# A recurrent-memory attention block on one core: steps padded to 3072 TensorE instructions per four, a transpose moved to DMA, and two reorderings at the last step

## The chip, the cores and the metric

The kernel runs on one core of one Trainium2 chip. The metric is the device time of one execution in microseconds; the kernel before takes 1007.62 us (median of three runs, 1007.40 to 1008.14). TensorE holds 128 x 128 cells. A product whose stationary operand has 32 columns uses a 128 x 32 strip of it, here called a tile; the four tiles 0, 32, 64 and 96 write the partitions 0-31, 32-63, 64-95 and 96-127 of a PSUM bank and can work side by side.

## What is computed

Two blocks run one after the other on x (2048 rows of 640). The first is attention over 64 segments of 32 rows; each segment sees its own rows and 8 memory rows, and its first 8 output rows are the memory of the next segment, so that the segments form a chain. The second is a gated feed-forward block.

```python
h = concat([mem, layernorm(x)[32*s : 32*s+32]])      # 40 rows
q, k, v = h @ Wq, h @ Wk, h @ Wv                     # 32 heads of 128
p = softmax(mask(q @ k.T * 128**-0.5))
o = (p @ v) @ Wo                                     # 40 rows of 640
mem, out[s] = o[:8], o[8:]
...
h = x + out
y = h + (relu(n @ W_gate) * (n @ W_up)) @ W_down     # n = layernorm(h), 1728 wide
```

## The kernel before, in words

**How it is written.** The code records operations in program order with what each reads and writes; `_Graph.solve` derives the waits. Within an engine the order is the written one, so nothing is scheduled: the order of the calls is the order of the instructions on each engine. An operation of TensorE ("pe") may hold many products.

**TensorE instructions.** `pe.matmul` makes two instructions, a weight load and a product. `again` (L357) makes a product without a load: it uses the weights that stand in the tile. One 32-column load with one 512-column product is the unit of the projections.

**A step.** The loop `for s in range(1, NSEG)` (L927) does segment s. `project` (L365) multiplies the 32 rows that are new to the step (8 of memory, 24 of x) by a half of Wk, Wq or Wv: five chunks c of 128 input features, and for each chunk four products of 512 columns, one on each tile (g = 0 to 3). `halves` says which half of the heads, `chunks` which chunks in which order, `ends` the chunks with which the PSUM sum starts and stops, and `held` that the first chunk uses `again`, since the half before has ended with the same weights. A step is, in order on TensorE:

1. K in two halves into banks P2 and P3 (L946), `pv_x` of step s-1 (32 small products, L654), Q in two halves into P0 and P1 (L967);
2. V half 0 with the scores of heads' half 0 between its chunks, V half 1 with the scores of half 1 (L979 to 1012; scores are 40-column products, L466);
3. `pv_mem` 0 (L519), `filler(0)`, `pv_mem` 1, `filler(1)`;
4. `wo_split` (32 products of 320 columns, L582), `wo_pass` (64 products of 160 columns, L565), which give the next step's memory, and `filler(2)`.

The fillers are work that does not hang on the chain. In the three steps with s % 4 = 2, 3, 0 they are a projection of other rows (`PARTS`); in the steps with s % 4 = 1 from 5 to 57 they are `woe_pass` (64 load-and-product pairs of 320 columns, L625, cut into 28, 8 and 28 by `WPARTS`). Step 62 has the latter too.

**LayerNorm 1.** Every fourth step (s % 4 = 1) the next normalised 128 rows are turned from rows to columns. For full blocks a transposing DMA on SP's queue does it (`flip_rows`, L347, issued at L991). The last block has 64 rows, in step 57: there TensorE turns them (`ln1_trans`, five loads and five products, L352) into bank BQ[1], and ScalarE copies them out (L1044). GpSimd then spreads them over the steps' operands (`ln1_back`).

**The last step.** Step 63 has no Q projection. After V half 1 it issues `merge_v` (the DMAs that arrange V for `pv_x`), the exponentials and the mask, `gate_up(0, 0)` (the feed-forward block's first two groups of five full-width products, L841), the scores of half 1, and leaves the loop (L996 to 1008). Behind the loop stand `rows(P3, ...)` (64 pairs of L625 for the rows of step 62, with a copy, a sum and two DMAs), `gate_up(0, 1)` and `pv_x` (L1167 to 1170). `gate_up` number i of block 0 writes banks i % 2 and 2 + i % 2; P3 is bank 7 and T0 bank 2.

Of the kernel before, what the change touches and what calls it, by code (L numbers as in the profile page):

```python
# [163 lines left out]
def build_kernel(nc, A_x, A_mem0, A_Wq, A_Wk, A_Wv, A_Wo, A_seg_len, B_W_gate, B_W_up, B_W_down, out):  # L164
    _, S, D = A_x.shape
# [6 lines left out]
    DC = D // 128  # L172
# [86 lines left out]
    def bank_bf(b):  # L259
        return ps[:, b * 512:(b + 1) * 512].bitcast(BF16)  # L260
# [14 lines left out]
    def B(n):  # L275
        return ("B", n)
# [68 lines left out]
    def flip_rows(dst, src, skey, dkey):  # L345

        add("sp", lambda e: e.dma_start_transpose(dst, src[:, :]), r=[skey], w=[dkey], dma=True)  # L347
# [14 lines left out]
            stop_tensor_calc=stop, tile_size=(128, 32 if g is not None else 128), tile_position=(0, 32 * (g or 0)),  # L362
            bass_skip_group_check=True, ldweights=False))

    def project(act, akeys, j, halves, banks, chunks=range(5), ends=(0, DC - 1), held=False):  # L365
        swap = 1 if j == 2 and akeys[0][0] == "acte" else 0

        def f(pe):
            for c in chunks:
                for n, i in enumerate(halves):  # L370
                    for g in range(4):
                        o = 2048 * i
                        w = (W[:, j, c, o + 512 * (g ^ swap):o + 512 * (g ^ swap) + 512] if j == 2 else
                             W[:, j, c, o:o + 2048].rearrange("p (h e) -> p h e", e=128)[:, :, 32 * g:32 * g + 32])
                        a = (bank(banks[n])[32 * g:32 * g + 32, :], act[:, c, :], w)
                        if n == 0 and not (held and c == chunks[0]):
                            ins = pe.matmul(*a, start=(c == ends[0]), stop=(c == ends[1]), skip_group_check=True)  # L377
                        else:
                            ins = again(pe, *a, c == ends[0], c == ends[1], g)
            return ins  # L380
        add("pe", f, r=list(akeys) + [("W", j, c) for c in chunks], w=[B(b) for b in banks] + [("Wdone", j)])
# [23 lines left out]
    def n_rows(b):  # L405
        return 64 if b < 0 else min(128, S - 64 - 128 * b)

    def ln1_load(b, buf, key, eng="sp"):
        t0, n = (0, 64) if b < 0 else (64 + 128 * b, min(128, S - 64 - 128 * b))
        dma(buf[0:n, :], x_ap[t0:t0 + n, :], w=[key], eng=eng)  # L410

    def ln1_trans(b, buf, key, bk):
        transpose_rows(buf, key, 64 if b < 0 else min(128, S - 64 - 128 * b), bk)
# [20 lines left out]
    def chunks_of(flat):  # L434
        return flat.rearrange("p (c t) -> p c t", t=128)
# [4 lines left out]
    def pass_act(s):  # L440
        p, j = place(s)
        return act_r[p][:, j], [("act", p, j, "m"), ("act", p, "x", j), ("act", p, "x")]
# [50 lines left out]
    def exp_x(s, hf):  # L493
        _, j = place(s)
        add("act", lambda a: a.activation(ap(Px, 128 * hf, [[256, 2], [32, 4], [1, 32]]), s_view(hf, M, M + SEG),
                                          ACTF.Exp, scale=SCALE), r=[B((P0, P1)[hf])], w=[("Px", hf)])
# [425 lines left out]
    row_stats(xl, ("xl",), n_rows(1))  # L922
    row_scale(xl, ("xl",), n_rows(1), xl, ("xl",))

    WAYS = ((range(DC),), (range(DC - 1, -1, -1), (DC - 1, 0), True))

    for s in range(1, NSEG):  # L927
        last = s == NSEG - 1
# [14 lines left out]
                woe_pass(BQ[0], WPARTS[n])  # L943
        if s > 0:
            a, ks = pass_act(s)
            for i in range(2):  # L946
                project(a, ks, 1, (i,), ((P2, P3)[i],), *WAYS[i])
                to_tok((P2, P3)[i], i, "act")
                if last and i == 1:
                    load_piece(("Ko", 0), "act")  # L950
                flip(i, Ko, i, [("Ko", i)])
            if s % 4 == 2 and more:
                row_std(n_rows(nb + 1))
                row_scale(xl, ("xl",), n_rows(nb + 1), xl, ("xl",), "pool")
            if s % 4 == 1 and e2 is not None:
                row_std(128)
                row_scale(xt, ("xt",), 128, xt, ("xt",), "pool")
            pv_x(s - 1, 0)
            norm_x(0)
            if s % 4 == 0 and e2 is not None:  # L960
                add_attn(xt[:, :], xt, at, [("xt",), ("at",), ("rx",)], [("xt",)], "pool")
                dma(h_d[128 * e2:128 * e2 + 128, :], xt[:, :], r=[("xt",)], w=[("h_d", e2)])
            if s % 4 == 2:
                merge_v(s, 1)
            if not last:
                for i in range(2):
                    project(a, ks, 0, (i,), ((P0, P1)[i],), *WAYS[i])  # L967
                    to_tok((P0, P1)[i], 2 + i, "act")
                    flip(2 + i, Qo, i, [("Qo", i)])
                    if i == 0:  # L970
                        norm_x_late(0)
                        flip_ox(s - 1, (0,))
            else:
                norm_x_late(0)
                flip_ox(s - 1, (0,))
            if s == NSEG - 2:
                dma(xn2T[0][:, :, :], xn2_d[:, :, :], r=[("xn2_d", u) for u in range(4)] + [("Wdone", 0)],
                    w=[("xn2", 0, u) for u in range(4)])
            project(a, ks, 2, (0,), (P2,), range(4), held=not last)  # L979
            scores(s, 0, (0, 1))  # L980
            project(a, ks, 2, (0,), (P2,), (4,))
            scores(s, 0, (2, 3))
            if not last:
                exp_mem(s, 0)
                mask_mem(s, 0)
            to_v(P2, Vp, 0, ("Vp",), "act")
            if last:
                load_piece(("Vp", 0), "act")
            if s % 4 == 1 and ln:
                if n_rows(nb) == 128:  # L990
                    flip_rows(chunks_of(at[:, :]), xl, ("xl",), ("at",))  # L991
                else:
                    ln1_trans(nb, xl, ("xl",), BQ[1])
                if more:
                    ln1_load(nb + 1, xl, ("xl",))
        if last:  # L996
            project(a, ks, 2, (1,), (P3,))
            to_v(P3, Vp, 1, ("Vp",), "act")
            merge_v(s, 0)
            flip_ox(s - 1, (1,))  # L1000
            exp_x(s, 0)
            gate_up(0, 0)
            scores(s, 1)
            exp_x(s, 1)
            load_piece(("g1", 0), "act")
            mask_x(s)
            late_o(s - 1)
            break
        project(a, ks, 2, (1,), (P3,), range(4))
        scores(s, 1, (0, 1))  # L1010
        project(a, ks, 2, (1,), (P3,), (4,))
        scores(s, 1, (2, 3))
        flip_ox(s - 1, (1,))
        if s == NSEG - 2:
            load_piece(("Pm", 0))
# [23 lines left out]
        if s > 0 and not woe and s != NSEG - 3:  # L1039
            late_o(s - 1)  # L1040
        if s % 4 == 1 and ln:
            n = n_rows(nb)
            if n < 128:
                copy_op("act", chunks_of(at[:, :])[:, :, 0:n], chunks_of(bank_bf(BQ[1])[:, 0:D])[:, :, 0:n], [B(BQ[1])],  # L1044
                        [("at",)])
            ln1_back(nb, chunks_of(at[:, :]), [("at",)], "pool")
        mask_x(s)
        if e2c is not None:
# [115 lines left out]
    def rowbuf(p):  # L1164
        return bass.AP((xl, xt)[p], 0, [[D, 64], [1, 320]])

    rows(P3, s % 2, s - 1)  # L1167
    gate_up(0, 1)
    load_piece(("hT", 0, 0))
    pv_x(s, P0)  # L1170
    norm_x(P0)
    norm_x_late(P0)
# [110 lines left out]
```

## Time and profile before

| | |
|---|---|
| three runs | 1007.40, 1007.62 and 1008.14 us |
| profiled execution | 1006.39 us |
| its span, first to last instruction | 1004.7 us; what lies around it is 1.69 us |
| TensorE products | 971.1 us busy, 97% of the span, 25153 instructions |
| TensorE weight loads | 495.7 us, 23308 instructions |
| VectorE, ScalarE, GpSimd | 712.9, 524.7 and 167.4 us |
| loop from the first `pv_x` to that of step 63 | 59.3 to 823.2 us |

The page gives each engine's busy time, the chain of work that ended last, the DMA queues and the costliest groups. A row of a group or of the timeline names the line, the operation and the tensors, with the number of instructions that follow each other (x20), their start and length, and in brackets the idle time of the engine just before and what ended it; "issue" there means that the profile shows nothing the engine waited for. Weight loads (PEld) have rows of their own and overlap products. Ends of products are modelled, so that busy rows overlap and starts are the better measure. The queue that the page calls "instruction" carries the program's own code to the engines.

### The profile page before, as it was taken

Reading aid. Unit: us, or ns where it says so; the run is one execution under the profiler, and the core shown is the slowest. Engines: PE = TensorE matmul, PEld = TensorE weight load, DVE = VectorE, ACT = ScalarE, POOL = GpSimd, SP = SyncE. Lnnn points to the kernel's source line nnn. Section 1 sums busy time; section 2 is a strip of 40 time slices with the busy share of each in tenths; the row PEclk is TensorE's granted clock in tenths of the full one; section 3 lists DMA queues with packets and bytes.
Section 4 is the critical chain, followed back from the end, with each engine's and each line's share of the span. In section 5 each row is a group of like instructions: output and inputs, shape, how many; then the busy total and the mean of one; then the engine's idle time right before and its main releaser. Section 6 shows DMA issues by size and latency. Waiting matters only on the chain.

```text
span 1004.7 us, 53813 instructions
## 1 busy us (share of the span) xinstructions
PE 971.1 (97%) x25153; PEld 495.7 (49%) x23308; DVE 712.9 (71%) x1863; ACT 524.7 (52%) x1331; POOL 167.4 (17%) x416
## 2 busy tenths in 40 slices
PE   3789999999999999999999999999999999999998
PEld 0245555555555554555555555555555555344443
DVE  2568787878878887888788878787878765445332
ACT  0456566556666666666666666665656643122121
POOL 7020202121302130222022212111110010000000
PEclk9999999999999999999999999999999999999999
DMA  9931212121212111121212131211111158413100
GB/s 373 418 102 28 53 28 55 33 55 50 53 41 54 49 53 47 47 54 47 53 41 63 47 55 40 41 41 38 40 29 40 38 165 251 108 20 92 27 14 26
DMA packets 72421, 73.01 MB, mean 73 GB/s; under 512 B 41632, under 2 KB 59008, under 8 KB 70272
## 3 DMA queue, kind: packets, MB, share of 16 engines
q1 hardware_dynamic: 70064, 68.27, 23.6%
q8 instruction: 190, 3.11, 1.3%
q10 hardware_dynamic: 2128, 1.31, 0.5%
q14 instruction: 39, 0.32, 0.1%
HBM read 37.04 MB, written 6.55 MB: 43 GB/s over the span
## 4 chain that ended last, share of the span: by engine, by line
PE 93%; SPq 3%; DMA 2%; issue 1%; DVE 1%; ACT 0%; POOL 0%; DVEq 0%; ACTq 0%
PE ps L377 43%; PE ps L841 11%; PE ps L359 10%; PE ps L565 7%; PE ps L582 6%; PE ps L625 4%; SPq L324 3%; PE ps L1088 3%; PE ps L466 2%; PE ps L654 2%; DMA Wo<-in_A_Wo_dram 2%; PE ps L519 2%; PE ps L854 0%; PE ps L1100 0%; DVE TBf L605 0%
## 5 line engine op out<-in xcount | busy, mean ns | idle before, releaser
L377 PE MATMUL ps<-W,act_r 128*32 128x512 bf16 x6832 | 447.4, 380 | 3.1 <-DVE act_r L606 1.8
L377 PEld LDWEIGHTS ps<-W,act_r 128*32 128x32 bf16 x6832 | 169.7, 96 | 212.0 <-issue 63.1
L401 ACT ACTIVATE tok<-ps 128x512 bf16<-128x512 f32 x190 | 109.3, 594 | 57.3 <-PE ps L377 48.8
L377 PE MATMUL ps<-W,act_e 128*32 128x512 bf16 x1224 | 120.0, 383 | 8.0 <-DMA W<-in_A_Wv_dram 3.7
L396 DVE STREAM_TRANSPOSE Ko<-tox 128x512 bf16<-128x512 bf16 x128 | 89.8, 703 | 42.7 <-ACT tox L401 41.5
L474 POOL COPY Qo<-Qe 128x256 bf16<-128x256 bf16 x64 | 28.0, 437 | 528.9 <-DVE oT L539 521.0
L401 ACT ACTIVATE tox<-ps 128x512 bf16<-128x512 f32 x134 | 79.6, 598 | 56.5 <-PE ps L377 35.5
L545 DVE STREAM_TRANSPOSE oT<-tox 128x512 bf16<-128x512 bf16 x128 | 89.8, 702 | 0.0
L396 DVE STREAM_TRANSPOSE Qo<-tok 128x512 bf16<-128x512 bf16 x124 | 85.6, 690 | 0.9
L565 PE MATMUL ps<-Wo,oT 128*32 128x160 bf16 x4032 | 82.3, 233 | 2.8 <-DMA Wo<-in_A_Wo_dram 1.7
L359 PE MATMUL ps<-W,act_e 128*32 128x512 bf16 x856 | 84.6, 385 | 0.0
L582 PE MATMUL ps<-Wo,oT 128*32 128x320 bf16 x2016 | 79.8, 299 | 0.5 <-DVE rm L529 0.5
L359 PE MATMUL ps<-W,act_r 128*32 128x512 bf16 x808 | 79.9, 382 | 0.0
L565 PEld LDWEIGHTS ps<-Wo,oT 128*32 128x32 bf16 x4032 | 71.8, 97 | 12.0 <-DMA Wo<-in_A_Wo_dram 2.8
L401 ACT ACTIVATE Vp<-ps 128x512 bf16<-128x512 f32 x127 | 75.2, 592 | 0.5 <-ACT Vp L401 0.5
L869 ACT ACTIVATE g<-ps 128x512 bf16<-128x512 f32 x52 | 30.1, 593 | 79.5 <-PE ps L841 79.5
L595 ACT ACTIVATE SA<-TA 64x40 f32<-64x40 f32 x126 | 29.5, 234 | 77.0 <-DVE TA L593 76.2
L841 PE MATMUL ps<-xn2T,Wu 128*128 128x512 bf16 x259 | 64.5, 379 | 0.1
L870 DVE TENSOR_TENSOR hT<-g,ps 128x512 bf16<-128x512 bf16 x52 | 35.7, 687 | 40.6 <-PE ps L841 38.6
L482 ACT ACTIVATE Pm<-ps 128x64 bf16<-128x64 f32 x126 | 28.1, 223 | 69.2 <-PE ps L466 69.2
L841 PE MATMUL ps<-xn2T,Wg 128*128 128x512 bf16 x247 | 61.8, 379 | 1.3 <-issue 1.0
L582 PEld LDWEIGHTS ps<-Wo,oT 128*32 128x32 bf16 x2016 | 53.9, 97 | 16.0 <-DVE rm L529 1.2
(116 smaller groups left out, 1463.1 us busy)
## 6 DMA issues: line engine op xcount, KB each, us to landing
VM<-Vp SPq DMA_DIRECT2D x126, 65.0 KB
VM<-Vp SPq DMA_DIRECT2D x63, 130.0 KB
W<-in_A_Wk_dram SPq DMA_DIRECT2D x5, 1024.0 KB
W<-in_A_Wq_dram SPq DMA_DIRECT2D x5, 1024.0 KB
W<-in_A_Wv_dram SPq DMA_DIRECT2D x5, 1024.0 KB
Wo<-in_A_Wo_dram SPq DMA_DIRECT2D x8, 640.0 KB
attn_d<-wtok SPq DMA_DIRECT2D x248, 7.5 KB
xt<-in_A_x_dram SPq DMA_DIRECT2D x16, 160.0 KB
```

What stands on the lines that cost most here:

```text
L324: add(eng, lambda e: e.dma_start(dst, src), r=r, w=w, dma=True)
L359: return pe.add_instruction(mybir.InstMatmult(name=nc.get_next_instruction_name(), engine=mybir.EngineType.PE, ins=[pe.lower_ap(rhs), pe.l ...
L377: ins = pe.matmul(*a, start=(c == ends[0]), stop=(c == ends[1]), skip_group_check=True)
L396: add("dve", lambda v: v.transpose(dst[:, 16 * i:16 * i + 16, 0:32], tok[t][:, :].rearrange("p (h f) -> p h f", f=32)), r=tok_keys(t), w=keys)
L401: add("act", lambda a: a.activation(dst, src, ACTF.Copy), r=r, w=w)
L545: add("dve", lambda v, kh=kh: v.transpose(ap(oT[p], 160 * kh + M, [[320, 4], [40, 4], [1, 32]]), ap(tox, 128 * kh, [[256, 4], [1, 4], [4, ...
L565: i = pe.matmul(bank(bk)[32 * gg:32 * gg + 32, 0:160], src[:, hb, 0:32], w[:, gg], start=(hb == CH[16 * halves[0]]), stop=(hb == CH[-1]), ...
L582: i = pe.matmul(bank(bk)[32 * q:32 * q + 32, 0:320], src[:, hb, 0:32], w, start=(n == 0), stop=(n == 7), skip_group_check=True)
L625: ins = pe.matmul(bank(bk)[32 * q:32 * q + 32, 0:320], src[:, hb, 0:32], w[:, 2 * (q % 2):2 * (q % 2) + 2], start=(i == 0), stop=(i == 15) ...
L841: ins = pe.matmul(bank(bk), w[:, c, lo:lo + 128], xn2T[par][:, c, :], start=(c == 0), stop=(c == DC - 1))
L870: add("dve", lambda v: v.tensor_tensor(hT[par][:, j, :], g1[gi][:, :], bank(bu), ALU.mult), r=[B(bu), ("g1", gi)], w=[("hT", par, j)])
L1088: i = pe.matmul(*a, start=(j == 0), stop=(j == FC - 1), skip_group_check=True)
```

## The change

1. **Divided products.** `project` gets `parts`, a number of instructions to add. A product of a chunk that does not start the sum is made as two products of 256 columns, each with its own load (two instructions more), or, for the last odd one, with one load for both (one more). The two halves stand behind each other, ahead of the next tile's product.
2. **Weights loaded again.** `held` is now given by step: of K half 1, Q half 1 and V half 0, up to three load the weights again (four loads each).
3. **The numbers.** `fill_of(s)` adds `FILL[s % 4]` = 56, 39, 8, 52 instructions (26 in step 1, none in 61 to 63), first by loads, the rest by divided products over K 0, K 1, Q 0 and Q 1. Four steps then have 12 x 256 = 3072 TensorE instructions (2917 before).
4. **The last 64 rows** of LayerNorm 1 take the same transposing DMA as the others; the five products and the copy go.
5. **Step 63:** V half 1 and the scores of half 1 stand as in every other step, then the exponentials and the mask, then `gate_up(0, 0)`.
6. **Behind the loop** `gate_up(0, 1)` stands ahead of `rows`, which now uses bank T0.

```diff
-    def project(act, akeys, j, halves, banks, chunks=range(5), ends=(0, DC - 1), held=False):
+    def project(act, akeys, j, halves, banks, chunks=range(5), ends=(0, DC - 1), held=False, parts=0):
...
+            left = parts
...
                         if n == 0 and not (held and c == chunks[0]):
-                            ins = pe.matmul(*a, start=(c == ends[0]), stop=(c == ends[1]), skip_group_check=True)
+                            k = min(left, 2) if c != ends[0] else 0
+                            left -= k
+                            for q in range(2 if k else 1):
+                                b = a if not k else (a[0][:, 256 * q:256 * q + 256], a[1],
+                                                     w[:, 256 * q:256 * q + 256] if j == 2 else w[:, 8 * q:8 * q + 8])
+                                if q and k == 1:
+                                    ins = again(pe, *b, c == ends[0], c == ends[1], g)
+                                else:
+                                    ins = pe.matmul(*b, start=(c == ends[0]), stop=(c == ends[1]), skip_group_check=True)
...
-    WAYS = ((range(DC),), (range(DC - 1, -1, -1), (DC - 1, 0), True))
+    WAYS = ((range(DC), (0, DC - 1)), (range(DC - 1, -1, -1), (DC - 1, 0)))
+    FILL = (56, 39, 8, 52)
+
+    def fill_of(s):
+        n = {1: 26, 57: 39, 61: 0, 62: 0, 63: 0}.get(s, FILL[s % 4])
+        alone = min(n // 4, 3)
+        rest = n - 4 * alone
+        return [k < 3 - alone for k in range(3)], [2 * ((rest // 2 + k) // 4) + (k == 0 and rest % 2) for k in range(4)]
...
+            held, parts = fill_of(s)
             for i in range(2):
-                project(a, ks, 1, (i,), ((P2, P3)[i],), *WAYS[i])
+                project(a, ks, 1, (i,), ((P2, P3)[i],), *WAYS[i], held=i == 1 and held[0], parts=parts[i])
...
-                    project(a, ks, 0, (i,), ((P0, P1)[i],), *WAYS[i])
+                    project(a, ks, 0, (i,), ((P0, P1)[i],), *WAYS[i], held=i == 1 and held[1], parts=parts[2 + i])
...
-            project(a, ks, 2, (0,), (P2,), range(4), held=not last)
+            project(a, ks, 2, (0,), (P2,), range(4), held=not last and held[2])
...
             if s % 4 == 1 and ln:
-                if n_rows(nb) == 128:
-                    flip_rows(chunks_of(at[:, :]), xl, ("xl",), ("at",))
-                else:
-                    ln1_trans(nb, xl, ("xl",), BQ[1])
+                flip_rows(chunks_of(at[:, :]), xl, ("xl",), ("at",))
...
+        project(a, ks, 2, (1,), (P3,), range(4))
+        scores(s, 1, (0, 1))
+        project(a, ks, 2, (1,), (P3,), (4,))
+        scores(s, 1, (2, 3))
         if last:
-            project(a, ks, 2, (1,), (P3,))
             to_v(P3, Vp, 1, ("Vp",), "act")
             merge_v(s, 0)
             flip_ox(s - 1, (1,))
             exp_x(s, 0)
+            exp_x(s, 1)
+            mask_x(s)
             gate_up(0, 0)
-            scores(s, 1)
-            exp_x(s, 1)
             load_piece(("g1", 0), "act")
-            mask_x(s)
             late_o(s - 1)
             break
...
-            n = n_rows(nb)
-            if n < 128:
-                copy_op("act", chunks_of(at[:, :])[:, :, 0:n], chunks_of(bank_bf(BQ[1])[:, 0:D])[:, :, 0:n], [B(BQ[1])],
-                        [("at",)])
...
-    rows(P3, s % 2, s - 1)
     gate_up(0, 1)
     load_piece(("hT", 0, 0))
+    rows(T0, s % 2, s - 1)
     pv_x(s, P0)
```

More of the change, by code (lines that the diff above doesn't have):

```diff
@@ L1001, in build_kernel @@
             exp_x(s, 0)
+            exp_x(s, 1)
+            mask_x(s)
             gate_up(0, 0)
-            scores(s, 1)
-            exp_x(s, 1)
             load_piece(("g1", 0), "act")
-            mask_x(s)
             late_o(s - 1)
             break
[L1009 to L1012, printed above, removed]
         flip_ox(s - 1, (1,))
```

## The prediction

> **What bounds the kernel now.** I read the page first: what ended last, and how many packets carry code.
>
> ```profile
> PE 971.1 (97%) x25153; PEld 495.7 (49%) x23308; DVE 712.9 (71%) x1863; ACT 524.7 (52%) x1331; POOL 167.4 (17%) x416
> ...
> q8 instruction: 190, 3.11, 1.3%
> ...
> PE 93%; SPq 3%; DMA 2%; issue 1%; DVE 1%; ACT 0%; POOL 0%; DVEq 0%; ACTq 0%
> ```
>
> TensorE's order is the time: 93% of the chain is its products, other engines hold it for some 2%. "issue" (0.7% in the chain's own view, 7 us) is time in which the profile shows nothing that it waited for. The code queue moved 190 packets of 16 KB, and TensorE has 48461 instructions: 255 a packet, so one packet is 256 instructions of TensorE.
>
> Next the timeline of TensorE by steps, from the first L654 row of a step to that of the next. Steps of one kind do the same work. The quiet ones last 12.03 us (s % 4 = 0, 2 and 3) and 12.18 (s % 4 = 1). Nine last longer: 5 by 0.41, 13 by 0.54, 17 by 0.24, 25 by 0.07, 32 by 0.53, 33 by 0.24, 37 by 0.10, 52 by 0.51, 53 by 0.92: 3.55 us in all. The worst one, step 53 (690.15 to 703.25), and beneath it the quiet step 49:
>
> ```profile
> 697.97 1.32 PE L565 MATMUL ps<-Wo,oT 128*32 128x160 bf16 x64
> 699.08 0.98 PE L625 MATMUL ps<-Wo,oTe 128*32 128x320 bf16 x21
> 700.71 0.45 PE L625 MATMUL ps<-Wo,oTe 128*32 128x320 bf16 x7 [0.65 <-issue]
> ```
>
> ```profile
> 649.17 1.28 PE L565 MATMUL ps<-Wo,oT 128*32 128x160 bf16 x64
> 650.28 1.13 PE L625 MATMUL ps<-Wo,oTe 128*32 128x320 bf16 x28
> 651.29 1.26 PE L377 MATMUL ps<-W,act_r 128*32 128x512 bf16 x20
> ```
>
> In step 53 the 28 equal products break after 21, and the loads break at the same place:
>
> ```profile
> 699.01 0.71 PEld L625 LDWEIGHTS ps<-Wo,oTe 128*32 128x32 bf16 x21
> 700.71 0.12 PEld L625 LDWEIGHTS ps<-Wo,oTe 128*32 128x32 bf16 x7 [0.99 <-issue]
> ```
>
> If I count the instructions of the built order (load, product and separate wait one each), all nine gaps stand at number 194 or 195 modulo 256. So these are page ends: the next 256 instructions are not there yet. With narrow windows of the DMA view I timed the packets. In step 53 the page before was entered at 696.59, the packet began at 697.90 (1.31 us later), took 1.53, and the first new instruction started 1.28 after its end: 4.12 us, for a page that quiet steps work off in 3.07. Elsewhere the start takes 0.9 to 1.4 after the page is entered near L582 (once 1.9), the packet 0.9 to 1.6, the rest 1.2 to 1.4: **3.65 us** at the means. A page of 512-column products lasts 4 to 6 us and hides this; only one that covers L582, L565 and what stands around them is shorter. Two things stay: the gap of 0.82 in step 62 (its page ends move by two instructions), and 0.29 in steps 11, 27 and 43, which wait for act_r.
>
> [...]
>
> **The change part by part.**
>
> *Periodic pages.* 3072 is 12 pages, so every fourth step has its page ends at the same instruction. From the built order of the changed kernel, with the same offset of 194, counted from the step's first L654 load: s % 4 = 1 at 202, 458, 714; 2 at 171, 427, 683; 3 at 193, 449, 705; 0 at 196, 452, 708. The nine gaps lose their places: **-3.55**.
>
> In kinds 2, 3 and 0 the middle end lies 0 to 2 instructions into L582, and the page lasts to the 41st or so instruction of the next K half, 3.9 to 4.1 us by quiet steps. The nine nearest pages of before (entered at 406 to 421) ended without a gap. At 3.65 needed, a late packet now and then: 42 steps x 0.015 = **+0.6** (0 to 2).
>
> In kind 1 it is otherwise. The page from 458 to 714 begins within `filler(1)` and ends 7 instructions before the end of `filler(2)`. In quiet steps these 256 instructions (436 to 692 of before) take **3.33 us**. The nearest ends of before are 671, 678 and 685: all three late, by 0.54, 0.24 and 0.92. At 725 and 732 (3.5 and 3.7 us, in the K half) none is late. Need less supply is 0.32; moving the three by their distance to 692 gives 0.46, 0.0 and 0.65, mean 0.37. I take 0.33 (0 to 0.6) in each of the 14 steps 5 to 57: **+4.6** (0 to 8.4). The K half waits behind, so it goes to the end.
>
> *Divided products.* The built order has 833 more products and 1479 more loads in the projections. Starts of one tile's products lie 215.6 ns apart at 512 columns and 135.6 at 320: 0.417 ns a column and 2.2 ns fixed. A division costs its tile 2.2 ns; four tiles run side by side, so between 833 x 2.2 / 4 = 0.46 and 833 x 2.2 = 1.8 us: **+0.7**, if a half holds up its own tile alone. No row shows two products of one tile behind each other; the other end is rival 2.
>
> *Loads instead of `held`.* A projection's load starts some 2 ns after the product before it on that tile and has 213 ns: 0. If that cover were gone, 97 ns a load.
>
> *Step 57.*
>
> ```profile
> 743.10 0.19 PE L466 MATMUL ps<-Qo,Ke 128*32 128x40 bf16 x4
> 743.23 0.32 PE L352 MATMUL ps<-ident,xl 64*128 64x64 bf16 x5
> 743.47 1.05 PE L377 MATMUL ps<-W,act_r 128*32 128x512 bf16 x16
> ```
>
> The next V half could start 0.02 after 743.10's last: 0.35 goes, which is all that step 57 is long (12.53 against 12.18): **-0.35**. The transposing DMA holds SP's queue for 1.25 us (median of 14), ahead of `merge_v`; in step 53 it is issued at 690.8, long before `merge_v`, and GpSimd reads its result at 698.5. I expect the same here.
>
> *Step 63.*
>
> ```profile
> 814.96 1.25 PE L377 MATMUL ps<-W,act_r 128*32 128x512 bf16 x20
> 816.37 1.03 PE L841 MATMUL ps<-xn2T,Wg 128*128 128x512 bf16 x4 [0.16 <-issue]
> ...
> 818.62 2.37 PE L625 MATMUL ps<-Wo,oT 128*32 128x320 bf16 x64
> 821.15 1.03 PE L841 MATMUL ps<-xn2T,Wg 128*128 128x512 bf16 x4 [0.16 <-issue]
> ```
>
> Entering full-width products costs 0.16 each time. The new order enters once less before `pv_x`: **-0.2**. `rows` must now wait until VectorE has emptied bank T0 after `gate_up(0, 0)`: ScalarE 0.60 and VectorE 0.69 behind the last product, and `gate_up(0, 1)` covers 2.15 us of that. `pv_x` keeps the same work ahead of it, so `merge_v` (issued 818.06) has as long to land; SP's later pieces follow `gate_up(0, 1)` as before. If that failed, about 1 us.
>
> Sum: -3.55 + 0.6 + 4.6 + 0.7 - 0.35 - 0.2 = **+1.8**, so 1006.39 becomes 1008.2 profiled; the median stands 1.23 above the profiled time: **1009.4**.
>
> **Rivals.**
>
> 1. *Kind 1 is not late.* Packets that start at a fixed place in the step might meet less traffic. For: the fastest parts seen (0.9, 0.9 and 1.2) give 3.0, under 3.33. Against: at this place of kind 1 `merge_v` is under way and packets took 1.16 to 1.53. Then +1.8 - 4.6 = -2.8, with kinds 2, 3 and 0 clean -3.4: **1004.4**.
> 2. *Halves hold the other tiles (slower).* If products start strictly in written order, the second half waits 107 ns for its tile and the next tile's product stands behind it. A wholly divided chunk then starts in 4 x 107 = 428 instead of 216 ns. Followed start by start through the four steps, 56 divisions cost 3.3 us; 14.5 times, +48: **1056**. It decides at the first divided product. Against it speak the scores:
>
> ```profile
> 742.71 0.19 PE L466 MATMUL ps<-Qo,Ko 128*32 128x40 bf16 x4
> 742.74 0.19 PE L466 MATMUL ps<-Qo,Ke 128*32 128x40 bf16 x4
> 742.76 0.19 PE L466 MATMUL ps<-Qo,Ko 128*32 128x40 bf16 x4
> ```
>
> Each four stand on tiles 0, 32, 64, 96, the next four on 32, 0, 96, 64. Fours start every 25 ns, single ones 3 ns apart. In written order a tile would be used again after 22 ns or 28 in turn, and half of its loads would start 2 ns before the product they must not disturb; by tiles it is 25 each time and the load 2 ns after, as in all projections. That is an argument, not a proof. [...]
> 3. *The page ends lie elsewhere than counted*, so that L565 takes them: each kind could be late by 0.5, 56 x 0.5 = +28, or none. The offset held for 190 packets; small.
>
> **How the numbers follow.** Forecast 0.47, rival 1 0.37, rival 2 0.12, rest 0.04. 0.2% is 2.0 us, about what a measurement of this kernel can tell from no change. Late kind 1 at 0 to 0.6 spreads the forecast from 1005 to 1013.5: slower 0.25, same 0.21, faster 0.01. Rival 1: faster 0.32, same 0.05. Rival 2 slower; the rest half slower, half same. Together faster 0.33, same 0.28, slower 0.39. The range joins forecast and rival 1, 1002.8 to 1013.5; rival 2 is left out.
>
> **What would show it.** Right: in the timeline of steps 5, 9, ... 57 the third group of L625 breaks at its 25th product (49th instruction) with an "issue" of a few tenths, while steps 6, 7, 8 stay at 12.03; no L352 after the start; one 0.16 less before L654 in step 63. Rival 1: L625 unbroken, kind 1 at 12.18. Rival 2: K and Q halves well above 1.09 us. Wrong altogether: a new wait in K or Q that names ScalarE or VectorE.

## The result, and the profile after

The changed kernel takes 1018.47 us (median of six runs, 1013.91 to 1021.46); the kernel before 1007.35 (six runs, 1005.17 to 1008.14). The ratio is 1.0111, with an interval of 1.0083 to 1.0140: slower by 11 us. The sign of the forecast holds, its size (+1.8) does not, and the range (to 1013.5) is missed by 5 us. The runs of the changed kernel spread over 7.5 us, those of before over 3.

The profiled execution took 1020.61 us, 1018.9 of them its span, 14.2 more than before; it lies 2 us above the median, so what follows accounts for 14 us and not for 11. From its page, the lines that answer to the three shown of before:

```profile
PE 979.6 (96%) x25995; PEld 541.8 (53%) x24782; DVE 717.2 (70%) x1863; ACT 524.8 (52%) x1330; POOL 168.2 (17%) x416
...
q8 instruction: 199, 3.26, 1.4%
...
PE 91%; SPq 3%; DMA 2%; DVE 1%; issue 1%; ACT 0%; POOL 0%; DVEq 0%; ACTq 0%
```

828 more products (the page shows 842, because 14 records are missing from the trace of before, all of them products of W_gate and W_up) add 8.5 us of "busy", which overlaps itself (in step 49 below the row of 660.92 ends at 662.25, the next one starts at 662.03) and is no loss of time by itself; there are 199 code packets in place of 190. What was lost stands in the view of the waits, where TensorE waited for nothing that the profile can name:

```profile
PE ps L634 <- issue: 8.8, 13, 0.9
```

L634 is `woe_pass` (L625 before), which runs in the loop only in kind 1 (s % 4 = 1) and step 62. In the kernel before that line read:

```profile
PE ps L625 <- issue: 1.0, 2, 0.7
```

Step 49, quiet before, now (its second page end at 659.7, its third at 663.8):

```profile
659.33 0.80 PE L634 MATMUL ps<-Wo,oTe 128*32 128x320 bf16 x8
659.84 1.38 PE L591 MATMUL ps<-Wo,oT 128*32 128x320 bf16 x32
660.92 1.33 PE L574 MATMUL ps<-Wo,oT 128*32 128x160 bf16 x61
662.03 0.30 PE L634 MATMUL ps<-Wo,oTe 128*32 128x320 bf16 x1
662.09 0.24 PE L574 MATMUL ps<-Wo,oT 128*32 128x160 bf16 x3
662.16 0.98 PE L634 MATMUL ps<-Wo,oTe 128*32 128x320 bf16 x23
663.79 0.32 PE L634 MATMUL ps<-Wo,oTe 128*32 128x320 bf16 x4 [0.65 <-issue]
```

24 of the 28 products of filler 2, then the break: the 25th is the first of a new page, as counted. The loads show that the page end before it, behind the first pair of filler 1, can be late as well:

```profile
659.68 0.12 PEld L634 LDWEIGHTS ps<-Wo,oTe 128*32 128x32 bf16 x7 [0.31 <-issue]
...
663.80 0.10 PEld L634 LDWEIGHTS ps<-Wo,oTe 128*32 128x32 bf16 x3 [0.99 <-issue]
```

All 14 steps of kind 1 from 5 to 57 have the second of these breaks; they last 13.04 us on average (12.43 to 13.73) against 12.18 quiet. By steps, from first `pv_x` row to first `pv_x` row, the loop is 13.5 us longer than before:

| part of the loop | longer than before |
|---|---|
| kind 1, steps 5 to 57 | +9.17 |
| kind 2, steps 6 to 58 | +2.14 |
| kind 3 | +0.54 |
| kind 0 (steps 32 and 52 shorter by 0.48 and 0.47) | +0.42 |
| steps 1 to 4 | +0.51 |
| steps 61 to 63 | +0.74 |

Step 57 (12.53 before, 13.31 now) has lost its transposes, as planned; V half 1 starts 0.02 us behind the scores' last four (755.00 and 755.02 in the timeline).

In step 63, `rows` and `pv_x` follow `gate_up` without a wait. The two 0.16 that stood ahead of L841 in the kernel before were no waits: the loads of the first such group are five where its row of products has four, so the record of its first product is missing.

```profile
816.13 0.76 PEld L841 LDWEIGHTS ps<-xn2T,Wg 128*128 128x128 bf16 x5 [0.42 <-DVE tox L672]
```

But in the changed kernel a page end now falls into the scores of step 63:

```profile
829.25 0.18 PE L475 MATMUL ps<-Qo,Ko 128*32 128x40 bf16 x3
829.87 0.18 PE L475 MATMUL ps<-Qo,Ko 128*32 128x40 bf16 x1 [0.43 <-issue]
829.87 0.20 PE L475 MATMUL ps<-Qo,Ke 128*32 128x40 bf16 x4
830.10 1.24 PE L850 MATMUL ps<-xn2T,Wg 128*128 128x512 bf16 x5
...
833.34 1.24 PE L850 MATMUL ps<-xn2T,Wu 128*128 128x512 bf16 x5
834.51 2.36 PE L634 MATMUL ps<-Wo,oT 128*32 128x320 bf16 x64
836.80 0.42 PE L663 MATMUL ps<-VM,Px 64*32 64x129 bf16 x32
```

### The profile page after: what moved, and what is told of

Read it like the earlier page. It is cut to its first block, busy times and chain, and to the rows that moved or that the text cites. A ratio compares the mean times of both kernels' runs of the same rounds, so it can differ in the third digit from the quotient of the medians.

```text
span 1018.9 us, 56128 instructions
## 1 busy us (share of the span) xinstructions
PE 979.6 (96%) x25995; PEld 541.8 (53%) x24782; DVE 717.2 (70%) x1863; ACT 524.8 (52%) x1330; POOL 168.2 (17%) x416
## 4 chain that ended last, share of the span: by engine, by line
PE 91%; SPq 3%; DMA 2%; DVE 1%; issue 1%; ACT 0%; POOL 0%; DVEq 0%; ACTq 0%
PE ps L386 46%; PE ps L850 10%; PE ps L359 7%; PE ps L574 7%; PE ps L591 6%; PE ps L634 4%; SPq L324 3%; PE ps L1096 3%; PE ps L475 2%; PE ps L663 2%; DMA Wo<-in_A_Wo_dram 2%; PE ps L528 2%; DMA Wd<-in_B_W_down_dram 0%; PE ps L863 0%; PE ps L1108 0%
## 5 line engine op out<-in xcount | busy, mean ns | idle before, releaser
L386 PE MATMUL ps<-W,act_r 128*32 128x512 bf16 (+1 forms) x8311 | 457.8, 359 | 3.0 <-DVE act_r L615 1.9
L386 PEld LDWEIGHTS ps<-W,act_r 128*32 128x32 bf16 x8311 | 216.1, 96 | 167.3 <-DVE act_r L615 30.2
L554 DVE STREAM_TRANSPOSE oT<-tox 128x512 bf16<-128x512 bf16 x128 | 94.3, 737 | 0.0
L574 PEld LDWEIGHTS ps<-Wo,oT 128*32 128x32 bf16 x4032 | 72.6, 97 | 9.6 <-DMA Wo<-in_A_Wo_dram 2.5
L850 PE MATMUL ps<-xn2T,Wg 128*128 128x512 bf16 x260 | 64.6, 379 | 0.0
L591 PEld LDWEIGHTS ps<-Wo,oT 128*32 128x32 bf16 x2016 | 55.6, 97 | 14.5 <-DVE rm L538 1.0
L475 PE MATMUL ps<-Qo,Ko 128*32 128x40 bf16 x2048 | 61.2, 181 | 0.4 <-issue 0.4
```

Of the source, the lines that this page charges most:

```text
L386: ins = pe.matmul(*b, start=(c == ends[0]), stop=(c == ends[1]), skip_group_check=True)
L475: i = pe.matmul(bank((P0, P1)[hf])[q:q + 32, o:o + 40], (Ko if a == 0 else Ke[p])[:, h, :], Qo[:, h, :], start=True, stop=True, skip_group ...
L554: add("dve", lambda v, kh=kh: v.transpose(ap(oT[p], 160 * kh + M, [[320, 4], [40, 4], [1, 32]]), ap(tox, 128 * kh, [[256, 4], [1, 4], [4, ...
L574: i = pe.matmul(bank(bk)[32 * gg:32 * gg + 32, 0:160], src[:, hb, 0:32], w[:, gg], start=(hb == CH[16 * halves[0]]), stop=(hb == CH[-1]), ...
L591: i = pe.matmul(bank(bk)[32 * q:32 * q + 32, 0:320], src[:, hb, 0:32], w, start=(n == 0), stop=(n == 7), skip_group_check=True)
L850: ins = pe.matmul(bank(bk), w[:, c, lo:lo + 128], xn2T[par][:, c, :], start=(c == 0), stop=(c == DC - 1))
```

## The experiments

In each run the page ends were counted as in the prediction (number 194 modulo 256) and their packets timed in the DMA view. I call **start** the time from the first instruction of a page to the beginning of the packet with the next page, **packet** its duration, **tail** the time from its end to the first instruction that it brings; the sum of the three is what a page **needs**. The **gap** is the time from the last load of a page to the first load of the next. A kind is late by what its steps last beyond the quiet ones (12.18 and 12.03 us). Measured times are medians of several executions; starts, packets, tails, gaps and steps come from one profile each, as means over the 14 steps of kind 1 where nothing else is said, at the third page end. "Before" is the kernel before on the same chip.

**The other parts alone.** No padding:

```diff
-    FILL = (56, 39, 8, 52)
+    FILL = (0, 0, 0, 0)
-        n = {1: 26, 57: 39, 61: 0, 62: 0, 63: 0}.get(s, FILL[s % 4])
+        n = FILL[s % 4]
```

> This is the changed kernel without its padding: no divided products, weights held as before (2917 TensorE instructions in four steps); the last 64 rows of LayerNorm 1 go by DMA and step 63 has its new order. Theory (the loss is code that comes late at the fixed page ends of kind 1, s % 4 = 1): it stands where the kernel before stands, with -0.35 in step 57 and -0.2 in step 63, and the page ends of the steps from 57 on dealt anew: 1006 to 1008 beside 1007.4 before. Rival (step 63 or the DMA costs something, as step 63 of the changed kernel took 0.55 us longer up to its first small product): 1 us or more above before, and the excess stands in step 57 or behind step 62. If the padding alone is guilty, none of the 11 us is seen here.

Measured 1007.38, before 1007.41; ratio 1.000 (0.9989 to 1.0010). Step 57 lasts 12.17 in place of 12.53. Step 62 is 0.35 shorter and step 63 0.47 longer, both with page ends that moved. So the 11 us belong to the padding.

**All page ends moved**, by more instructions in steps 1 and 2:

```diff
-        n = {1: 26, 57: 39, 61: 0, 62: 0, 63: 0}.get(s, FILL[s % 4])
+        n = {1: 140, 2: 60, 57: 39, 61: 0, 62: 0, 63: 0}.get(s, FILL[s % 4])
```

> The changed kernel with 166 more instructions in steps 1 and 2 (140 and 60 in place of 26 and 8), so that from step 3 on every page end stands 166 instructions earlier in its step: kind 1 at 36, 292 and 548 in place of 202, 458 and 714, the others near 5 to 30, 261 to 286 and 517 to 542. In the kernel before, steps whose ends lay there had no gap, and packets had 0.4 us or more to spare. Theory (position): kind 1 falls from 13.04 to 12.2 us a step, kinds 2, 3 and 0 to 12.03 to 12.08; the loop loses 12 to 15 us against the changed kernel, and the time is 1003 to 1005.5. Rival 1 (each added instruction or divided product costs, wherever the pages end): 1017 to 1020, as it has as many of them and 166 more. Rival 2 (code comes at a limit of some 4 us a page, 12 pages in 48.2 us, so that a shift only moves the gaps elsewhere): 1012 or more, with gaps at other places.

Measured 1005.40, before 1007.41; ratio 0.9976 (0.9966 to 0.9985). With the changed kernel's padding in the steps 3 to 60, and 166 instructions more in steps 1 and 2, it is 13 us faster than that kernel. Kind 1 lasts 12.17 to 12.24, kind 2 12.03, kind 3 12.04 (12.33 in steps 11, 27 and 43, as before), kind 0 12.04 to 12.13. The timeline of step 49, where nothing breaks:

```profile
648.77 1.28 PE L574 MATMUL ps<-Wo,oT 128*32 128x160 bf16 x64
649.88 1.12 PE L634 MATMUL ps<-Wo,oTe 128*32 128x320 bf16 x28
650.90 1.26 PE L386 MATMUL ps<-W,act_r 128*32 128x512 bf16 x20
```

Both rivals fall: neither the instructions nor the divided products cost the 11 us, the place of the page ends does. What the divided products do cost is seen in the same steps: +0.13, +0.04, +0.30 and +0.62 in kinds 1, 2, 3 and 0 against their quiet time, 1.1 us in 56 steps. One gap is left, in step 62 (13.78 in place of 13.17).

**Kind 1 alone moved:**

```diff
-    FILL = (56, 39, 8, 52)
+    FILL = (56, 0, 47, 52)
-        n = {1: 26, 57: 39, 61: 0, 62: 0, 63: 0}.get(s, FILL[s % 4])
+        n = {1: 26, 2: 8, 61: 0, 62: 0, 63: 0}.get(s, FILL[s % 4])
```

> The changed kernel with the 39 added instructions of kind 1 moved into the following step, ahead of that step's second page end (56, 0, 47, 52 in place of 56, 39, 8, 52): as many instructions in four steps, and page ends of the kinds 3 and 0 where they were; in kind 1 the second and third page end stand 39 products and loads later in the work, 475 and 731 in place of 458 and 714, one behind the start of the 32 products of 320 columns, the other in the K half. Steps 21 and 41 of the kernel before had their ends at 469, 725 and 476, 732 and no gap. Theory (position): kind 1 falls from 0.86 to 0.0 to 0.3 late, kinds 2, 3 and 0 stay as they are: 1018.5 - 14 x 0.56 to 0.86 = 1006.5 to 1010.6. Rivals (instructions or divided products cost wherever they stand; the tail of the kernel): 1016 to 1020.

Measured 1016.72; ratio 1.0085 (1.0068 to 1.0101). A miss: kind 1 lasts 12.78, 0.60 late in place of 0 to 0.3, and the scores of step 63 stand still for 1.25. By the time alone no difference from the changed kernel can be told, since the two intervals overlap. Filler 2 is whole again, but K behind it breaks:

```profile
658.08 1.12 PE L634 MATMUL ps<-Wo,oTe 128*32 128x320 bf16 x28
...
660.36 1.89 PE L386 MATMUL ps<-W,act_r 128*32 128x512 bf16 x33 [0.43 <-issue]
```

The page needs 1.33 + 1.26 + 1.38 = 3.97, and the 256 instructions from 475 to 731 last about 3.4 us (3.97 less the 0.60). Two steps of before without a gap at this place (their pages lasted 3.5 and 3.7, since their K was not divided) had been luck, not proof.

**Thirteen pages in four steps:**

```diff
-    FILL = (56, 39, 8, 52)
+    FILL = (120, 103, 72, 116)
-        n = {1: 26, 57: 39, 61: 0, 62: 0, 63: 0}.get(s, FILL[s % 4])
+        n = {1: 140, 2: 124, 61: 0, 62: 0, 63: 0}.get(s, FILL[s % 4])
```

> Padding to 13 pages of 256 in four steps (3328 instructions; 64 more in each step, nearly all by divided products of K and Q, 2774 more products than before in place of 833), page ends otherwise as in the kernel with all pages moved. A page then has 48.2 / 13 = 3.71 us on average, against the 3.6 to 4.1 that one needs from entering a page to the first instruction of the next. Theory with a limit (code comes one page after the other, each needing about 3.9): up to 13 x 0.2 = 2.5 us per four steps late, +20 to +40 us, 1027 to 1047, with gaps in all kinds. Theory by position alone (only pages that hold the dense part of kind 1 are late): the two pages with 3.4 and 3.1 us are late by 0.3 to 1.0 in 14 steps, +4 to +18: 1010 to 1024. Divided products alone, at 2 ns each: +6, 1010.

Measured 1047.19; ratio 1.0384 (1.0359 to 1.0409). Now every kind is late, and `wo_pass` and the projections wait far more than in the kernel before (1.1 and 0.6 us there, in two places each):

```profile
PE ps L574 <- issue: 12.0, 14, 1.4
...
PE ps L386 <- issue: 6.5, 19, 0.7
```

Steps of the four kinds last 12.58, 12.16, 12.96 and 13.32, 51.0 in all: 3.93 us a page on average, where the work of quiet steps gives 3.71. Position alone (1010 to 1024) and divided products alone (1010) fall. A limit of about 3.9 us a page fits, and twelve pages of 4.02 us would just keep below it, so that the place decides. It is not proved: single steps of kinds 1 and 2 are still quiet (12.19 and 12.05), and late pages at many places would add up to the same average.

**The same place, reached by leaving out**, and steps 61 to 63 padded too:

```diff
-        n = {1: 26, 57: 39, 61: 0, 62: 0, 63: 0}.get(s, FILL[s % 4])
+        n = {1: 0, 2: 0, 3: 0, 4: 52, 61: 40, 62: 52, 63: 100}.get(s, FILL[s % 4])
```

> The same page ends as in the run with all pages moved, but reached the other way round: 90 instructions less in steps 1 to 4 (0, 0, 0 and 52 added in place of 26, 8, 52 and 56) instead of 166 more; and steps 61, 62 and 63 get 40, 52 and 100 added instructions, so that the page ends of step 62 lie where they lie in kind 1 (44, 300, 556), and that of step 63 at 213, in the stretch of full-width products. Theory (position): steps 5 to 60 as in that run (12.03 to 12.19 us); step 62, which lasted 13.79 there with one gap of 1.72 at its third page end, falls to 12.1 to 12.3; step 63 up to its first small product from 9.99 to 9.7 or 9.8; the pre-loop part, 0.6 longer there, returns to 59.4: 1005.4 - 1.5 - 0.2 - 0.6 = 1003.1, range 1002 to 1004.5. Rival (added instructions cost by themselves): 1005 or more, as 192 are added in the last three steps.

Measured 1006.65, before 1007.65; ratio 0.9989 (0.9980 to 0.9998), 2 us above the range. Steps 5 to 60 are as quiet as was said; step 62 is the miss, 14.72 in place of 12.1 to 12.3, and step 63 10.66. One of its gaps, and the DMA view of the 5 us before (busy share of the engines in 40 slices, in tenths):

```profile
807.17 1.22 PE L574 MATMUL ps<-Wo,oT 128*32 128x160 bf16 x58 [1.46 <-issue]
```

```profile
DMA  9205931099907304578969979978899999999997
...
q1 hardware_dynamic: 958, 1.26, 85.1%
q8 instruction: 1, 0.02, 1.2%
```

The page was entered at 802.07; its successor's packet began 2.87 us later, among 958 packets of data (weights and rows for the feed-forward block), and took 0.97. So a code packet began late here, in a stretch in which data kept the DMA engines busy for 85.1% of the time. That the data holds it up fits, but no run changes the data of step 62 alone.

**No transfer of V in kind 1:**

```diff
-        merge_v(s, 0)
+        if s % 4 != 1 or s < 5:
+            merge_v(s, 0)
         pv_mem(s, 0)
```

Kind 1 also gets 41 added instructions in place of 39, for two separate waits that go with the transfers.

> The changed kernel, page ends at the same instructions (two more added in kind 1, since two separate waits go), but in the steps 5, 9, ... 57 the transfers of merge_v are left out: pv_x of these steps then works on older V, which changes the output and not the work of TensorE. At 7 to 9 us of each step these transfers keep 5 to 11 of 16 DMA engines busy, just when the packet for the third page end comes. Theory (the packet is late because of that traffic: 1.25 us in place of 0.95, and a later start): kind 1 is late by 0.3 to 0.55 instead of 0.86, that is 1018.5 - 4.5 to 8 = 1010.5 to 1014. Rival (the page is too dense, whatever the traffic): kind 1 stays at 0.75 to 0.95 late, 1017 to 1019.

Measured 1015.72; ratio 1.0083 (1.0064 to 1.0102). Kind 1 is 0.55 late; packets took 0.99 in place of 1.24, starts were 1.27 in place of 1.43. The time lies between the theory's range and the rival's, 1.7 above the one and 1.3 below the other, and its interval overlaps that of the changed kernel. What speaks for the theory are the packets and the 0.55, the upper end of its range, and they are those of one profile.

**No wait ahead of the page end:**

```diff
-    WPARTS = (range(0, 7), range(7, 9), range(9, 16))
+    WPARTS = (range(0, 10), range(10, 12), range(12, 16))
```

> The changed kernel with the 16 fillers of kind 1 and step 62 cut 10, 2, 4 instead of 7, 2, 7 (pairs: 40, 8, 16 in place of 28, 8, 28). No page end moves, but the second one, at 458, then lies within the first filler and no longer 18 instructions behind the wait for the probabilities (the wait in front of pv_mem 1). Theory (a wait right before the page end takes away the head start with which the next packet is asked for): in kind 1 the packet begins 0.3 to 0.9 after the page is entered in place of 1.2 to 1.4, and the third page end is late by 0 to 0.5; what is then seen in its place is a wait for act_r in front of K, since the last filler is 0.5 us shorter: 1011 to 1016. Rival (the packet begins 1.2 or more behind the page's entry whatever stands ahead): still 0.86 late, and the wait for act_r is hidden behind it: 1017.5 to 1020.

Measured 1017.22; ratio 1.0103 (1.0079 to 1.0126): by the time no difference that can be told from the changed kernel. In the profile kind 1 is 0.50 late. Packets began 0.79 to 1.00 after the page's entry in 7 steps, 1.23 to 1.59 in the other 7. In six of the first seven the page's own packet had ended 1.86 us or more ahead of its use, in six of the others 1.75 or less. Of the 0.50 late code is only about half. With filler 2 cut to 16 products, K behind it waits for `act_r` (the next step's rows, which VectorE writes), and no step of kind 1 is below 12.41, 0.23 above quiet. In step 17, where the packet began after 0.79 and the products do not break, the loads of K show it:

```profile
266.40 0.77 PEld L386 LDWEIGHTS ps<-W,act_r 128*32 128x32 bf16 x20 [0.31 <-DVE act_r L615]
```

**As the run by leaving out, with the last steps as before:**

```diff
-        n = {1: 26, 57: 39, 61: 0, 62: 0, 63: 0}.get(s, FILL[s % 4])
+        n = {1: 0, 2: 0, 3: 0, 4: 52, 61: 92, 62: 0, 63: 0}.get(s, FILL[s % 4])
```

> As the run that reached the moved page ends by 90 instructions less in steps 1 to 4, but with 92 added instructions in step 61 and none in 62 and 63, so that the page ends of the last two steps lie as in the kernel before (16, 272, 528 in step 62 and 5, 261 in step 63). There the loads of the second half of the kernel keep 11 to 17 DMA engines busy from 3 to 11 us of step 62, and code packets began 1.7 to 2.9 us after the page was entered; an extra page end in that stretch cost 0.9 and 0.9 more. Theory (page ends under traffic): step 62 falls from 14.7 to 13.0 to 13.3, step 63 up to its first small product from 10.7 to 9.9 to 10.3, steps 5 to 60 stay at 12.03 to 12.2: 1006.65 - 2 to 2.5 = 1004.2 to 1004.7, which would be the fastest of all. Rival (that run was slower than the first one with moved pages for another reason, such as the later steps 1 to 4): 1006 to 1007 again.

Measured 1005.49, before 1008.14; ratio 0.9971 (0.9959 to 0.9983). Step 62 lasts 12.87, step 63 10.40. This run and the first one with moved pages beat the kernel before by 2.6 and 2.0 us, the run by leaving out by 1.0; all three have the same page ends in steps 5 to 60. The 1004.2 to 1004.7 that I gave is missed by 0.8; before took 0.5 more here than beside the run that I had started from.

**Both single edits** (no V transfer, fillers 40, 8, 16):

> The changed kernel with both single edits of before: merge_v left out in the steps 5, 9, ... 57 (pv_x of these steps works on older V), and fillers cut 40, 8, 16. Theory (the time from entering a page to the next page's first instruction is a sum of start, packet and tail, and each edit takes its own part): start 0.85, packet 1.0, tail 1.4, that is 3.25 against a page of 2.98 to 3.03: kind 1 is 0.2 to 0.35 late, packets begin below 1.0 in most of its steps, and the time falls below both single runs (1015.7 and 1017.2): 1009 to 1013. Rival (the two are one and the same, or a wait for act_r takes the place): no lower than 1014.5.

Measured 1017.83; ratio 1.0094 (1.0076 to 1.0113). A miss by the time. Start 1.19, packet 1.12 and tail 1.40 make 3.71 in place of 4.09, but from its entry to its last load the page lasts only 2.86 (3.10 in the changed kernel): what makes a page quicker takes away some of the time in which the next one comes. Kind 1 is 0.50 late, as with the fillers alone, and no step of it is below 12.41: the wait for `act_r` again. The time says little of kind 1 here, because steps 1 and 2 of the profiled execution are 2.9 us longer than in that of the changed kernel; a page end in step 1 came 1.1 late.

**A longer page ahead of the dense one:**

```diff
+        for _ in range(5 if s % 4 == 1 and 5 <= s <= 57 else 0):
+            project(a, ks, 2, (1,), (P3,), (0,), held=True)
         project(a, ks, 2, (1,), (P3,), range(4))
...
-    FILL = (56, 39, 8, 52)
+    FILL = (56, 19, 8, 52)
...
-        n = {1: 26, 57: 39, 61: 0, 62: 0, 63: 0}.get(s, FILL[s % 4])
+        n = {1: 26, 61: 0, 62: 0, 63: 0}.get(s, FILL[s % 4])
```

> The changed kernel with 20 products of 512 columns more in the steps 5, 9, ... 57, ahead of V half 1 (they fill the bank that V half 1 then starts anew, so the result is the same), and 20 added instructions less ahead of them: 3072 in four steps as before. The second and third page end of kind 1 stand at the same instructions of the same work (the second behind the first pair of filler 1, the third before the last four products of filler 2); only the page that lies before, which has 256 instructions in 3.04 us, now lasts 1.08 us longer. Quiet kind 1 is then 12.18 + 1.08 = 13.26. Theory (packets come one after the other, each asked for only when the page before it has been entered, at 3.6 to 4.1 each; kind 1 is late because two dense pages follow each other, 3.04 and 3.15, and the head start at the first of them is used up): with a first page of 4.1 the packet for the third page end begins earlier behind the entry of its page, below 0.9, and the gap falls from 0.9 to 0 to 0.4: kind 1 at 13.3 to 13.65 us, 1022 to 1027. Rival (the dense page alone, 3.15 against a need of 4.1, whatever lies ahead of it): the gap stays at 0.8 to 1.0, kind 1 at 14.0 to 14.3, 1032 to 1036.

Measured 1032.72; ratio 1.0242 (1.0217 to 1.0268). My theory falls, and the rival's numbers are met but for 0.03: kind 1 at 14.10, gap 1.03. The page's own packet had mostly ended 2 us ahead of its use, yet no start was below 1.18.

**The longer page, and no wait ahead of the end** (the edits of the run above and of the fillers 40, 8, 16):

> The run with the longer page before (20 products of 512 columns more) and the fillers of kind 1 cut 40, 8, 16 as in the run without the wait before the page end. In that run the packet for the third page end began 0.8 to 1.0 us behind its page's entry where the packet before had ended 1.85 us or more ahead of its use, and 1.2 to 1.4 where not; in the run with the longer page alone packets arrived early, but a wait stood ahead of the page, and none began before 1.18. Theory (the next packet is asked for when TensorE's front end enters the page; it runs ahead of the work only if the page is there in time AND no wait holds it): with both, packets begin 0.4 to 0.95 behind the entry in at least 11 of 14 steps; the gap falls from 1.03 to 0.3 to 0.6, kind 1 from 14.10 to 13.4 to 13.7, the time from 1032.7 to 1023 to 1028. Rival (the start is 1.2 or more at this place in any case): 1030 to 1034.

Measured 1028.25; ratio 1.0193 (1.0176 to 1.0210), just above the theory's range and below the rival's. Starts are 0.81 to 0.99 in 12 of 14 steps (up to 0.95 in 10; I had said at least 11), median 0.88 in place of 1.32; start, packet and tail make 3.68 in place of 4.14, the gap is 0.69 in place of 1.03. Kind 1 lasts 13.67, but eight of its steps stand at 13.49 to 13.51, held by the wait for `act_r` behind the short filler. The same break of filler 2 in step 49, first with the longer page alone, then with no wait ahead of its end (16 products there, since filler 2 is shorter):

```profile
675.06 1.00 PE L634 MATMUL ps<-Wo,oTe 128*32 128x320 bf16 x24
676.99 0.32 PE L634 MATMUL ps<-Wo,oTe 128*32 128x320 bf16 x4 [0.93 <-issue]
```

```profile
669.53 0.58 PE L634 MATMUL ps<-Wo,oTe 128*32 128x320 bf16 x12
670.69 0.32 PE L634 MATMUL ps<-Wo,oTe 128*32 128x320 bf16 x4 [0.58 <-issue]
```

So with the longer page, and no wait just ahead of the page end, the next packet begins some 0.4 us earlier: 0.88 in place of 1.32. The cause that the theory gives is not shown by the profile. In kind 1 of the changed kernel the wait for the probabilities stands 18 instructions ahead of the page end, and packets begin 1.43 behind the entry; that the wait holds them up there is the author's reading.

**And no V transfer:**

> The kernel of the run before this one, and merge_v left out in the steps 5, 9, ... 57 as well (pv_x of these steps works on older V; two added instructions make up for two waits that go). Theory (start, packet and tail are a sum): the packet takes 1.0 in place of 1.24 as in the run without merge_v, so the time from entry to the next page is 0.7 + 1.0 + 1.4 = 3.1 against a page of 2.9 to 3.0: the gap falls to 0.1 to 0.35, kind 1 to 13.2 to 13.45, the time to 1019 to 1024. Rival (as where the two edits stood together without the longer page, nothing is added up): no lower than the run before this one.

Measured 1028.75; ratio 1.0206 (1.0189 to 1.0222). A miss: no gain by the time; in the profile kind 1 is 0.09 shorter. Its theory could not have been met in any case: eight of the 14 steps stand at 13.49 to 13.51, above the 13.2 to 13.45 that I gave, since K waits for `act_r`. In step 13 (208.44 to 221.93) the loads of K show it, with the code in time:

```profile
219.66 0.77 PEld L386 LDWEIGHTS ps<-W,act_r 128*32 128x32 bf16 x20 [0.63 <-DVE act_r L615]
```

So this run does not decide what the packets' time is worth. Packets took 1.14, though no data moved on this core from 7 to 11 us of these steps. What makes a packet last 0.9 or 1.4 us, and why one in five starts 1.9 to 2.1 after its page's entry in kind 1 of the changed kernel, stays open.

## Why the prediction was wrong

**The step that failed** is "3.65 us at the means", the time that a page needs, set against 3.33 of supply. The mechanism, the place and the instruction at which the loads break were right. The 3.33 holds: in step 5 the two page ends are 4.10 apart, and the step is 0.77 longer than a quiet one; in the run with all pages moved the same 256 instructions last 3.33. But in the 14 steps of kind 1 start, packet and tail took 1.43 + 1.24 + 1.42 = **4.09**. The packet lies within what the prediction had seen elsewhere (0.9 to 1.6); start and tail, on average, lie just above the upper ends of theirs (0.9 to 1.4 and 1.2 to 1.4). The three pages of before that ended nearest to this place, in steps 13, 33 and 53, needed 4.03, 3.44 and 4.12, 3.86 on average. The prediction did use these three, by how late they were (mean 0.37 when moved to the place), and that so small a sample agreed with 0.32 was chance: of the 14 pages of the changed kernel only two need less than 3.8. Why this place needs more is shown in part, by the start, which fell from 1.32 to 0.88 once the wait just ahead of it was moved (the two runs with the longer page); the rest stays open.

- **Kind 1**, +4.6 (0 to 8.4): measured (13.04 - 12.18) x 14 = 12.0. 0.76 a step is 4.09 less 3.33, 0.1 is the second page end, late by some 0.2 to 0.5 in steps 13, 33 and 49, which I had not counted at all: the page ahead of it lasts only 3.04.
- **Kinds 2, 3 and 0**, +0.6 (0 to 2): about 3.7, that is 2.45 in kind 2, 1.0 in kind 0 and 0.25 in kind 3, steps 2 to 4 included and what the divided products cost taken off. They needed 4.01, 4.01 and 3.95, not 3.65, and kind 2 is late by 0.1 to 0.4 in most steps. The supply was mis-sized as well: in the run with moved pages these 256 instructions last 3.78, 3.88 and 3.77, below the 3.9 to 4.1 of the prediction, while in the kernel before, from the same start, they last 4.2 to 4.3. Divided products use up a page sooner.
- **Nine gaps vanish**, -3.55: right in 32 and 52 (0.48 and 0.47 shorter) and, in the runs with moved pages, in all others; in the changed kernel seven of the nine are kind 1, and six of them got a larger one (step 53 has 0.31 in place of 0.92).
- **Divided products**, +0.7 (0.46 to 1.8): 1.1. Right.
- **Step 57**, -0.35: right (0.36 in the run without padding), hidden here behind its late page.
- **Step 63**, -0.2: the reordering is worth 0.14, as the run with thirteen pages shows, whose step 63 has no late page (9.73 against 9.87). The working was wrong all the same: 0.16 "each time" was the missing record of a product, not a wait, so that the size came near by luck. By the starts of loads and products before, I estimate 0.09 us on the way from 32-column to full-width products (816.04 to 816.13) and 0.09 on the way back (818.31 to 818.40). In the changed kernel the step is 0.80 longer. I had counted page ends for the steps of the loop's four kinds, not for 62 and 63.
- **`held` to loads at 0**: kind 2, which has only such additions, lasts 12.03 in the run with moved pages. Right.

The measured terms (-3.55, 12.0, 3.7, 1.0 for divided products outside kind 1, -0.35, and 0.74 in steps 61 to 63) make 13.5, as the loop has it.

**Rivals.** Kind 1 not late: refuted in all 14 steps; the fastest parts (3.0) never came together. Halves that hold the other tiles: refuted; 784 divided products in the steps 5 to 60 cost 1.1 us, where this rival gave 3.3 in every four steps, 46 in all. Nor do products here start strictly in written order: in the rows of step 49 above the first product of filler 2 starts at 662.03, 60 ns ahead of the last three of `wo_pass`, which are written before it. Seven steps of kind 1 show this, by 20 to 60 ns.

## What to carry to other kernels

Count the instructions of an engine that is busy all the time into pages, and set the time of every page against the time that the next one needs at that very place; in kind 1 of the changed kernel that was 3.6 to 4.4 us, and a stretch of short operations that runs through a page faster (in 3.33 us there) has to share it with long ones. Fixing the page ends to the loop makes every repetition equal, for better or worse: 13 us lay between two phases of the same padding, so try the phase on the chip, or count it by rows of the place itself, before the padding is judged. Dividing products made the pages that hold them shorter in time (3.77 to 3.88 us in the run with moved pages, 4.2 to 4.3 before). And keep page ends away from waits, which was worth 4.5 us in the one pair of runs that shows it; that they should keep out of heavy transfers is likely and not proved here. A run that shortens the work behind a wait can meet the next wait instead, as four runs did with `act_r`: look for it before a missing gain is taken as an answer.

## What the runs showed of the hardware

- With 13 pages in four steps a page took 3.93 us on average, though the work would have been done in 3.71. Whether code delivery has a rate of its own, or late pages at many places add up, no run separates.
- At the third page end of step 62, where 958 data packets moved in 5 us of one run, the code packet began 1.5 to 2.9 us after its page was entered; in kind 1 of the changed kernel mostly 1.2 to 1.4.
- In the steps 5 to 60 of all runs no packet began more than 1.0 us before the first instruction of the page ahead of it, and behind the dense page of kind 1 (the changed kernel and its variants with that page) none earlier than 0.76 us after it, even where that page had arrived 2 us ahead of its use. In the changed kernel TensorE stands still at one line, L634, 13 times for 8.8 / 13 = 0.68 us on average.
- One page end cost different amounts from execution to execution: the same one in step 1 broke nothing in the profile of the changed kernel and cost 0.7 to 1.4 us in four others with the same step 1. The changed kernel's six executions spread over 7.5 us, the ten of the run with all pages moved over 2.2 (1004.37 to 1006.54); four with a late page in K spread over 1.8, so that late code is not shown to be the cause.
